# Loading q, k and v by whole batches instead of half batches in a fused sliding-window attention and soft-MoE kernel

## The chip, the cores and the metric

One core of a Trainium2 chip runs the whole kernel. The metric is the device time of one execution in microseconds (us); lower is better. Verdicts are ratios: the mean time of one kernel's fast runs divided by the mean time of the other's fast runs of the same rounds, with a 95% interval. They are therefore not quite the ratio of the medians that are quoted beside them. A profile is one execution; single executions of the same kernel differ, mostly by up to about 0.5%.

## The reference

Eight batches of eight heads, 576 tokens, head size 64. Each token attends to itself and the 63 tokens before it. The result, as 4608 rows of 512, goes through a soft mixture of eight experts with four slots each.

```python
def reference(q, k, v, phi, w1, w2):                  # cut and joined
    scores = scale * q @ k.T                          # per batch and head
    scores = where((rel >= 0) & (rel < 64), scores, -1e9)
    attn = softmax(scores) @ v                        # (8, 8, 576, 64)
    x = attn.transpose(0, 2, 1, 3).reshape(4608, 512)
    logits = x @ phi                                  # (4608, 32)
    slot_in = softmax(logits, axis=0).T @ x           # 32 slots
    for e in range(8):                                # 4 slots each
        slot_out[e] = relu(slot_in[e] @ w1[e]) @ w2[e]
    return softmax(logits, axis=1) @ slot_out
```

The inputs are float32 in HBM: 28.3 MB of q, k and v and 33.6 MB of weights. The output is 9.4 MB.

## The kernel before

The kernel works in 16 units of half a batch (four heads). All q, k, v and weight loads but the first three are DMAs issued by GpSimd, which cast float32 to float16 on the way (the software queue, q0). A partition of SBUF takes nine consecutive tokens of one head:

```python
    T = 9
    pld = ctx.enter_context(tc.tile_pool(name="pld", bufs=3))
    ...
    def src_of(u, i):
        b, half = units[u]
        return (q, k, v)[i][b, 4 * half:4 * half + 4].rearrange(
            "(x h) (g t) d -> (h g) x (t d)", x=2, h=2, t=T)

    def load_part(u, i):
        ...
        t = pld.tile([128, 2, S], FP16, name=nm, tag=nm)
        if u:                                            # unit 0 comes by the SP queue
            nc.gpsimd.dma_start(out=t, in_=src_of(u, i))  # 128 x 2 runs of 9*64 values
```

Each run of 9 x 64 values is one DMA packet of 1152 bytes (counted where it is written, in float16). The TensorEngine then transposes the tokens (stage `t1`), computes scores, and so on. The expert weights follow in the same queue; those of the last two experts' w2 come by column halves, so that the first half of the output columns can be combined and stored while the second half is still loading:

```python
            for _ in range(2 if u % 4 == 3 else 1):      # weights between the units
                load_w(*w_order.pop(0))
    ...
            if e > E - NLAST:
                stir(8)                                  # warming matmuls while PE waits
            expert_o(e, 0)
```

The softmax here doesn't subtract the row's maximum and nothing guards it: scores larger than these inputs give would overflow.

## Time and profile before

| | before |
|---|---|
| time, median | 181.57 us in the first 4 runs, 181.61 us in 16 runs with the later ones |
| span of the profiled run | 179.5 us |
| software queue | 22496 packets, 30.09 MB, 6.0 to 154.9 us |
| q, k, v packets of 1152 bytes | 11520 |
| attention done, experts begin | 133 us |
| last weight lands | 155.2 us |
| last store packet ends | 178.2 us |

The page of the kernel before, from the views of forty equal slices (busy share in tenths; GB/s is what all DMA engines moved) and of DMA queues (packets, MB, summed time of the packet records as a share of 16 engines' span):

```profile
...
PE   2559879968998797999978999887879947698200
...
DMA  5999999999999999999999999999999999999994
GB/s 199 287 209 202 206 210 212 208 205 213 209 213 202 209 213 208 209 207 210 211 205 213 207 213 206 213 213 218 205 217 214 204 196 179 332 376 408 429 422 183
...
q0 software_dynamic: 22496, 30.09, 94.8%
q1 hardware_dynamic: 6000, 11.21, 16.5%
q8 instruction: 23, 0.38, 0.8%
...
```

The DMA row is full in all but the edge slices; PE is nearly full too up to slice 30, but it ends attention in time and then waits. Loads run at some 209 GB/s, stores (slices 37 to 39) at 408 to 429.

The windows view of the same run, three stretches in which q, k, v and weights stream in:

```profile
...
core 0: us, PE busy (x) PEld busy (x) DVE busy (x) ACT busy (x) POOL busy (x), PEclk, DMA share, GB/s
20.00:60.00 40.00, 35.48 (x887) 27.43 (x885) 30.95 (x72) 32.48 (x53) 16.40 (x24) 1.00 1.17 209
60.00:100.00 40.00, 34.87 (x839) 26.66 (x838) 30.37 (x68) 31.52 (x55) 15.56 (x23) 1.00 1.16 209
100.00:130.00 30.00, 26.71 (x606) 20.08 (x607) 23.67 (x55) 21.78 (x38) 8.83 (x14) 1.00 1.13 211
...
```

The DMA share is above 1: the records of neighbouring packets on one engine overlap, so a record's length is not what a packet costs. That is the point on which the prediction turns.

The chain of work that ended last, in order of time (start us, length us, what):

```profile
...
98.47 13.99 DMA kn<-in_k_dram
112.75 19.50 DMA w2s<-in_moe_w_dram
132.53 0.88 POOL w2s L89
...
135.03 20.18 DMA w2l<-in_moe_w_dram
155.25 0.42 PE sop L522 x8
...
```

From 98 us the chain is DMA alone. Every load waits for 13 to 20 us behind about eight others in the queue; the last one lands at 155.2, and the matmul that waited for it runs at 155.25. Before 98 us the chain runs mostly through compute on PE, ACT and DVE, but the DMA row is full there too: with some eight loads in the queue, a load that is issued a little later doesn't leave the DMA engines idle.

### The profile page before, as it was taken

What the parts mean: (1) busy time and instruction counts of PE and PEld (TensorE: products, weight loads), DVE (VectorE), ACT (ScalarE), POOL (GpSimd) and SP (SyncE); (2) the same over time, 40 slices, a digit from 0 to 9 for tenths busy, and PEclk for the clock granted to TensorE, in tenths of its full rate; (3) what the DMA queues carried; (4) which work ended last, traced back from release to release, by engine and by line L of the source; (5) the groups of instructions that cost most, each with busy time, mean ns of one, the idle gap of its engine ahead of it and who ended that gap; (6) DMA issues with size and microseconds to landing.
All of it is one profiled execution on the core that took longest, in us unless ns stands there. A gap on an engine that the chain in (4) does not pass through costs nothing.

```text
span 179.5 us, 6676 instructions
## 1 busy us (share of the span) xinstructions
PE 139.8 (78%) x2929; PEld 102.1 (57%) x2929; DVE 114.1 (64%) x274; ACT 116.4 (65%) x203; POOL 55.2 (31%) x86
## 2 busy tenths in 40 slices
PE   2559879968998797999978999887879947698200
PEld 0448658647765676766757767675657724343000
DVE  5634969858949668886777886887842212589400
ACT  3556779787696777968769779694642313689400
POOL 8644534434343442524344333322131000000000
PEclk9999999999999999999999999999999997969955
DMA  5999999999999999999999999999999999999994
GB/s 199 287 209 202 206 210 212 208 205 213 209 213 202 209 213 208 209 207 210 211 205 213 207 213 206 213 213 218 205 217 214 204 196 179 332 376 408 429 422 183
DMA packets 28524, 41.71 MB, mean 232 GB/s; under 512 B 2128, under 2 KB 21584, under 8 KB 28496
## 3 DMA queue, kind: packets, MB, share of 16 engines
q0 software_dynamic: 22496, 30.09, 94.8%
q1 hardware_dynamic: 6000, 11.21, 16.5%
q8 instruction: 23, 0.38, 0.8%
q14 instruction: 5, 0.04, 0.1%
HBM read 61.93 MB, written 9.44 MB: 398 GB/s over the span
## 4 chain that ended last, share of the span: by engine, by line
DMA 34%; PE 34%; ACT 15%; issue 6%; DVE 3%; SPq 0%; POOL 0%; ACTq 0%; POOLq 0%
DMA w2l<-in_moe_w_dram 11%; DMA w2s<-in_moe_w_dram 11%; PE tr L164 10%; DMA kn<-in_k_dram 8%; ACT pm L227 5%; DMA first<-in_v_dram 4%; PE sc L215 4%; PE tr L193 4%; PE sc L222 4%; ACT ob L553 4%; PE tr L290 3%; PE av L253 3%; PE cp L549 3%; ACT kT L171 2%; PE lt L383 2%
## 5 line engine op out<-in xcount | busy, mean ns | idle before, releaser
L227 ACT ACTIVATE pm<-sc 128x1024 f16<-128x1024 f32 (+1 forms) x48 | 40.1, 835 | 18.6 <-PE sc L222 18.5
L215 PE MATMUL sc<-rep,hide 64*128 64x512 f16 (+1 forms) x96 | 18.1, 340 | 6.3 <-ACT pm L227 3.8
L261 DVE TENSOR_TENSOR x_bp<-av,rc 128x512 f16<-128x512 f32 x32 | 22.1, 690 | 1.0
L253 PE MATMUL av<-vw,pm 128*64 128x65 f16 x576 | 19.5, 197 | 3.7 <-issue 3.5
L171 ACT COPY qT<-tr 128x640 f16<-128x640 f16 (+1 forms) x31 | 21.2, 745 | 1.3 <-PE tr L164 1.3
L171 ACT COPY kT<-tr 128x640 f16<-128x640 f16 (+1 forms) x31 | 21.8, 785 | 0.2 <-PE tr L164 0.2
L222 PE MATMUL sc<-qT,kT 64*128 64x64 f16 x576 | 19.0, 193 | 0.6 <-issue 0.5
L555 DVE TENSOR_SCALAR ob<-cp,crcp 128x256 f32<-128x256 f32 (+1 forms) x25 | 13.9, 588 | 8.0 <-PE cp L549 7.9
L253 PEld LDWEIGHTS <-pm 128*64 128x64 f16 x576 | 16.0, 112 | 4.6 <-issue 3.9
L222 PEld LDWEIGHTS <-kT 64*128 64x128 f16 x576 | 15.4, 96 | 5.2 <-issue 1.4
L259 DVE RECIPROCAL rc<-av 128x8 f32<-128x8 f32 x32 | 6.4, 201 | 15.7 <-PE av L253 15.7
L66 POOL DMA_DIRECT2D vn<-in_v_dram x15 | 10.8, 720 | 15.3 <-PE sc L222 3.4
L553 ACT ACTIVATE ob<-cp,crcp 128x256 f32<-128x256 f32 (+1 forms) x26 | 13.7, 563 | 2.6 <-PE cp L549 1.7
L66 POOL DMA_DIRECT2D qn<-in_q_dram x15 | 10.8, 719 | 14.9 <-PE tr L204 4.0
L86 POOL DMA_DIRECT2D w1s<-in_moe_w_dram x16 | 8.8, 552 | 20.3 <-DMA w2s<-in_moe_w_dram 12.7
L549 PE MATMUL cp<-slot_oa,ET 128*128 128x256 f16 (+1 forms) x51 | 12.7, 348 | 2.8 <-ACT ob L553 1.1
L169 DVE COPY vT<-tr 128x512 f16<-128x512 f16 x16 | 11.6, 722 | 5.2 <-PE tr L164 5.2
L164 PE MATMUL tr<-ident,kn 128*64 128x128 f16 x288 | 13.7, 234 | 1.3 <-issue 1.2
L164 PE MATMUL tr<-ident,vn 128*64 128x128 f16 x288 | 12.6, 228 | 2.5 <-ACT vn L432 2.5
L66 POOL DMA_DIRECT2D kn<-in_k_dram x15 | 10.8, 718 | 11.1 <-PE tr L164 4.4
L171 ACT COPY vT<-tr 128x640 f16<-128x640 f16 x16 | 12.9, 809 | 1.5 <-PE tr L164 1.5
L164 PE MATMUL tr<-ident,qn 128*64 128x128 f16 x288 | 12.1, 233 | 1.7 <-ACT qn L432 1.7
(109 smaller groups left out, 241.5 us busy)
## 6 DMA issues: line engine op xcount, KB each, us to landing
w1s<-in_moe_w_dram POOLq DMA_DIRECT2D x16, 512.0 KB, 14.8
w2s<-in_moe_w_dram POOLq DMA_DIRECT2D x14, 512.0 KB, 14.8
out_dram<-ob SPq DMA_DIRECT2D x6, 768.0 KB, 7.5
qn<-in_q_dram POOLq DMA_DIRECT2D x15, 288.0 KB, 13.0
kn<-in_k_dram POOLq DMA_DIRECT2D x15, 288.0 KB, 13.0
vn<-in_v_dram POOLq DMA_DIRECT2D x15, 288.0 KB, 13.0
out_dram<-ob SPq DMA_DIRECT2D x8, 384.0 KB, 4.8
w2l<-in_moe_w_dram POOLq DMA_DIRECT2D x2, 512.0 KB, 19.9
```

Of the source, the lines that this page charges most:

```text
L66: nc.gpsimd.dma_start(out=t, in_=src_of(u, i))
L164: nc.tensor.transpose(tr[64 * x:64 * x + 64, j, :], src[:, x, 64 * (t0 + j):64 * (t0 + j) + 64], ident[:, :])
L169: nc.vector.tensor_copy(out=o, in_=i)
L171: nc.scalar.copy(out=o, in_=i)
L215: nc.tensor.matmul(sc[:, x, 0:128 * n], hide[64 * x:64 * x + 64, :], rep[64 * x:64 * x + 64, 0:2 * n, :], start=True, stop=False, skip_gro ...
L222: nc.tensor.matmul(sc[:, x, o:o + 64], st["kT"][64 * x:64 * x + 64, h, 64 * i:64 * i + 128], st["qT"][64 * x:64 * x + 64, h, 64 * i:64 * i ...
L227: nc.scalar.activation(pm[:, :, 0:2 * n, :], sc[:, :, 0:128 * n].rearrange("p x (w q) -> p x w q", q=64), AF.Exp, scale=scale)
L253: nc.tensor.matmul(av[r0:r0 + 64, kk, 65 * (w // 2):65 * (w // 2) + 65], pm[:, x, h * n + w, :], st["vw"][:, i, 2 * h + x, 0:65], start=Tr ...
L261: nc.vector.tensor_tensor(out=xb[:, c0:c0 + 2, 256 * half:256 * half + 256].rearrange("p c (k d) -> p k c d", d=64), in0=avv[:, :, :, 0:64 ...
L549: nc.tensor.matmul(cp[:, :], ET[:, bp, j::T], slot_oa[:, cols], start=True, stop=True)
L553: nc.scalar.activation(ob[:, g, :], cp[:, :], AF.Copy, scale=cr)
L555: nc.vector.tensor_scalar(out=ob[:, g, :], in0=cp[:, :], scalar1=cr, scalar2=None, op0=ALU.mult)
```

## The change

The change loads a whole batch at a time: 18 tokens of one head per partition, so a packet is 2304 bytes and there are half as many. Half as many DMAs are issued as well. The rest of the diff follows from that: two batches of buffers instead of three units, transposes by batch, a permuted order of the heads in x (undone in phi and in one final add), half-size w2 tiles that take over the freed buffers, and more warming matmuls near the end. The core of the diff, cut:

```diff
     T = 9            # still used for the first batch and the output
+    T2 = 18
-    pld = ctx.enter_context(tc.tile_pool(name="pld", bufs=3))
+    pld = ctx.enter_context(tc.tile_pool(name="pld", bufs=2))
...
-    def load_part(u, i):
-        t = pld.tile([128, 2, S], FP16, name=nm, tag=nm)
-            nc.gpsimd.dma_start(out=t, in_=src_of(u, i))
+    def load_batch(b):
+        for i in range(3):
+            t = pld.tile([128, 2, T2 * 64], FP16, name=names[i], tag=names[i])
+            nc.gpsimd.dma_start(out=t, in_=(q, k, v)[i][b].rearrange(
+                "(x h) (g t) d -> (h g) x (t d)", x=2, t=T2))
...
+        elif n >= 2 and (e, n - 2) not in w2_t:
+            tag = names[(2 * (e - E + 4) + n - 2) % 3]      # late w2 halves reuse q, k, v buffers
+            w2_t[e, n - 2] = pld.tile(...)
...
-            if u + 1 < nu:
-                stage_t1(u + 1, j)
+            if u == 0:
+                stage_t1_unit(1, j)                         # second half of batch 0
+            elif u == 1:
+                stage_t1(1, 2 * j)                          # all of batch 1 in one unit
+                stage_t1(1, 2 * j + 1)
+            elif b < B:
+                stage_t1(b, 3 * (u % 2) + j)
...
-            if e > E - NLAST:
-                stir(8)
+            if e >= E - NLAST:
+                stir(16 if e == E - 1 else 8)
```

(The comments are added here.)

More of the change, by code (lines that the diff above doesn't have):

```diff
@@ L34 @@
     T = 9
-    G = S // T
+    T2 = 18
     NW = S // 64
@@ L38 @@
     NFC = F // 128
+    PERM = (0, 2, 1, 3)
     scale = 1.0 / float(Dh) ** 0.5
@@ L42 @@
     gap.tile([128, 64], FP16, name="gap")
-    pld = ctx.enter_context(tc.tile_pool(name="pld", bufs=3))
+    pld = ctx.enter_context(tc.tile_pool(name="pld", bufs=2))
     pxb = ctx.enter_context(tc.tile_pool(name="pxb", bufs=2))
     pw1 = ctx.enter_context(tc.tile_pool(name="pw1", bufs=8))
-    pw2 = ctx.enter_context(tc.tile_pool(name="pw2", bufs=7))
+    pw2 = ctx.enter_context(tc.tile_pool(name="pw2", bufs=E - 4))
     const = ctx.enter_context(tc.tile_pool(name="const", bufs=1))
@@ L54, with src0, w2_of @@
     units = [(b, half) for b in range(B) for half in range(2)]
+    nu = len(units)
     loaded = {}
-    def src_of(u, i):
-        b, half = units[u]
-        return (q, k, v)[i][b, 4 * half:4 * half + 4].rearrange(
-            "(x h) (g t) d -> (h g) x (t d)", x=2, h=2, t=T)
-    def load_part(u, i):
-        nm = ("qn", "kn", "vn")[i]
-        t = pld.tile([128, 2, S], FP16, name=nm, tag=nm)
-        if u:
-            nc.gpsimd.dma_start(out=t, in_=src_of(u, i))
-        loaded[u, i] = t
-    def load_unit(u):
+    names = ("qn", "kn", "vn")
+    def src0(half, i):
+        return (q, k, v)[i][0].rearrange("(x r h) (g t) d -> r (h g) x (t d)", x=2, r=2, t=T)[half]
+    def load_batch(b):
         for i in range(3):
-            load_part(u, i)
+            t = pld.tile([128, 2, T2 * 64], FP16, name=names[i], tag=names[i])
+            nc.gpsimd.dma_start(out=t, in_=(q, k, v)[i][b].rearrange(
+                "(x h) (g t) d -> (h g) x (t d)", x=2, t=T2))
+            loaded[b, i] = t
     w1_t, w2_t = {}, {}
     NLAST = 2
+    def w2_of(e, f, cols):
+        if e >= E - NLAST:
+            return w2_t[e, cols.start // (D // 2)][:, f, :]
+        return w2_t[e, f // 4][:, f % 4, cols]
     def load_w(e, n):
@@ L78, in load_w @@
             w1_t[e] = pw1.tile([128, NHD, F], FP16, name="w1s", tag="w1s")
-        if n == 2:
-            if e < E - 1:
-                w2_t[e] = pw2.tile([128, NFC, D], FP16, name="w2s", tag="w2s")
-            else:
-                w2_t[e] = pxb.tile([128, NFC, D], FP16, name="w2l", tag="x_bp")
+        cols = e >= E - NLAST
+        if n == 2 and (e < E - 4 or e == E - 1):
+            if e < E - 4:
+                t = pw2.tile([128, NFC, D], FP16, name="w2s", tag="w2s")
+            else:
+                t = pxb.tile([128, NFC, D], FP16, name="w2l", tag="x_bp")
+            for m in range(2):
+                w2_t[e, m] = t[:, :, D // 2 * m:D // 2 * m + D // 2] if cols else t[:, 4 * m:4 * m + 4, :]
+        elif n >= 2 and (e, n - 2) not in w2_t:
+            tag = names[(2 * (e - E + 4) + n - 2) % 3]
+            w2_t[e, n - 2] = pld.tile([128, NFC, D // 2] if cols else [128, NFC // 2, D], FP16,
+                                      name="w2h", tag=tag)
         if n < 2:
@@ L86, in load_w @@
             nc.gpsimd.dma_start(out=w1_t[e][:, c], in_=moe_w1[e].rearrange("(p c) f -> p c f", p=128)[:, c])
-        elif e >= E - NLAST:
+        elif cols:
             c = slice(D // 2 * (n - 2), D // 2 * (n - 1))
-            nc.gpsimd.dma_start(out=w2_t[e][:, :, c], in_=moe_w2[e].rearrange("(c p) d -> p c d", p=128)[:, :, c])
+            nc.gpsimd.dma_start(out=w2_t[e, n - 2], in_=moe_w2[e].rearrange("(c p) d -> p c d", p=128)[:, :, c])
         else:
             g = slice(2 * n - 4, 2 * n - 2)
-            nc.gpsimd.dma_start(out=w2_t[e].rearrange("p (g c) d -> p g (c d)", c=2)[:, g],
+            nc.gpsimd.dma_start(out=w2_t[e, n - 2].rearrange("p (g c) d -> p g (c d)", c=2),
                                 in_=moe_w2[e].rearrange("(g p c) d -> p g (c d)", p=128, c=2)[:, g])
@@ L104 @@
         first.append(pw1.tile([128, 2, S], FP32, name="first", tag="w1s"))
-        nc.sync.dma_start(out=first[i], in_=src_of(0, i))
+        nc.sync.dma_start(out=first[i], in_=src0(0, i))
     ident = const.tile([128, 128], FP16, name="ident")
@@ L116 @@
     nc.vector.tensor_copy(out=hide[64:128, :], in_=m)
-    load_unit(0)
-    load_unit(1)
+    for i in range(3):
+        loaded[0, i] = pld.tile([128, 2, 2, T * 64], FP16, name=names[i], tag=names[i])
+        nc.gpsimd.dma_start(out=loaded[0, i][:, 1], in_=src0(1, i))
     rep = const.tile([128, 8, 64], FP16, name="rep")
@@ L128 @@
     for n in range(2):
-        kt = const.tile([128, 2, 64 + S], FP16, name=f"kT{n}")
-        vt = const.tile([128, 2, 64 + S], FP16, name="vT") if n == 0 else vTs[0]
+        kt = const.tile([128, 4, 64 + S], FP16, name=f"kT{n}")
+        vt = const.tile([128, 4, 64 + S], FP16, name="vT") if n == 0 else vTs[0]
         vw = const.tile([128, NW, 4, 66], FP16, name=f"vw{n}")
-        for h in range(2):
+        for h in range(4):
             nc.vector.memset(kt[:, h, 0:64], 0.0)
@@ L157, with t1 @@
     ps = psum1.enter_context(tc.tile_pool(name="ps", bufs=2, space=bass.MemoryType.PSUM))
-    def t1(src, dst, engines):
-        for (t0, n), eng in zip(((0, 5), (5, 4)), engines):
+    def t1(src, dst, pieces, engines):
+        nh = dst.shape[1]
+        nt = src.shape[2] // 64
+        for (t0, n), eng in zip(pieces, engines):
             tr = ps.tile([128, 8, 128], FP16, name="tr", tag="tr", bufs=4)
@@ L165, in t1 @@
                                         src[:, x, 64 * (t0 + j):64 * (t0 + j) + 64], ident[:, :])
-            o = dst.rearrange("p h (g t) -> p h g t", t=T)[:, :, :, t0:t0 + n]
-            i = tr[:, 0:n, :].rearrange("p t (h g) -> p h g t", h=2)
+            o = dst.rearrange("p h (g t) -> p h g t", t=nt)[:, :, :, t0:t0 + n]
+            i = tr[:, 0:n, :].rearrange("p t (h g) -> p h g t", h=nh)
             if eng is nc.vector:
@@ L173, with t1_dst, stage_t1_unit, stage_t1 @@
     state = {}
-    def stage_t1(u, which):
-        if which == 0:
-            qT = pqt.tile([128, 2, S], FP16, name="qT", tag="qT")
-            state[u] = dict(qT=qT, kT=kTs[u % 2], vT=vTs[u % 2], vw=vws[u % 2])
-            t1(loaded[u, 0], qT, (nc.scalar, nc.scalar if u else nc.vector))
-        elif which == 1:
-            t1(loaded[u, 1], state[u]["kT"][:, :, 64:64 + S], (nc.scalar, nc.scalar if u else nc.vector))
-        else:
-            t1(loaded[u, 2], state[u]["vT"][:, :, 64:64 + S], (nc.scalar, nc.vector))
+    byb = {}
+    def t1_dst(b, which):
+        if b not in byb:
+            byb[b] = (pqt.tile([128, 4, S], FP16, name="qT", tag="qT"), kTs[b % 2], vTs[b % 2])
+        return byb[b][which][:, :, 64:64 + S] if which else byb[b][which]
+    def stage_t1_unit(u, which):
+        engines = (nc.scalar, nc.vector) if u == 0 or which == 2 else (nc.scalar, nc.scalar)
+        t1(loaded[0, which][:, u], t1_dst(0, which)[:, 2 * u:2 * u + 2], ((0, 5), (5, 4)), engines)
+    def stage_t1(b, n):
+        which, part = divmod(n, 2)
+        engines = (nc.scalar, nc.vector) if which == 2 or b == 1 and part == 1 else (nc.scalar, nc.scalar)
+        if b == 1 and n == 4:
+            engines = (nc.vector, nc.vector)
+        t1(loaded[b, which], t1_dst(b, which), ((9 * part, 5), (9 * part + 5, 4)), engines)
+    def open_unit(u):
+        b, half = units[u]
+        qT, kT, vT = byb[b]
+        r = slice(2 * half, 2 * half + 2)
+        state[u] = dict(qT=qT[:, r], kT=kT[:, r], vT=vT[:, r], vw=vws[u % 2])
     def steps(j):
@@ L212, in stage_s @@
         n = len(wins)
-        sc = ps.tile([128, 2, 512], FP32, name="sc", tag="sc", bufs=1)
+        apart = False
+        if apart:
+            sc = [ps.tile([128, 512], FP32, name=f"sc{x}", tag="tr", bufs=4) for x in range(2)]
+        else:
+            sct = ps.tile([128, 2, 512], FP32, name="sc", tag="sc", bufs=1)
+            sc = [sct[:, x] for x in range(2)]
         for x in range(2):
-            nc.tensor.matmul(sc[:, x, 0:128 * n], hide[64 * x:64 * x + 64, :],
+            nc.tensor.matmul(sc[x][:, 0:128 * n], hide[64 * x:64 * x + 64, :],
                              rep[64 * x:64 * x + 64, 0:2 * n, :], start=True, stop=False,
@@ L221, in stage_s @@
                     o = 64 * (h * n + w)
-                    nc.tensor.matmul(sc[:, x, o:o + 64],
+                    nc.tensor.matmul(sc[x][:, o:o + 64],
                                      st["kT"][64 * x:64 * x + 64, h, 64 * i:64 * i + 128],
@@ L226, in stage_s @@
         pm = ppm.tile([128, 2, 8, 64], FP16, name="pm", tag="pm")
-        nc.scalar.activation(pm[:, :, 0:2 * n, :],
-                             sc[:, :, 0:128 * n].rearrange("p x (w q) -> p x w q", q=64),
-                             AF.Exp, scale=scale)
+        if apart:
+            for x in range(2):
+                nc.scalar.activation(pm[:, x], sc[x][:, :].rearrange("p (w q) -> p w q", q=64),
+                                     AF.Exp, scale=scale)
+        else:
+            nc.scalar.activation(pm[:, :, 0:2 * n, :],
+                                 sct[:, :, 0:128 * n].rearrange("p x (w q) -> p x w q", q=64),
+                                 AF.Exp, scale=scale)
         st["pm", j] = pm
@@ L332, in fin_ex @@
             for kk in range(NHD):
-                nc.tensor.matmul(fin["sums"][:, 1, NSLOT * c:NSLOT * c + NSLOT], fin_x(b, kk, c), phi_sb[:, kk, :],
+                nc.tensor.matmul(fin["sums"][:, 1, NSLOT * c:NSLOT * c + NSLOT], fin_x(b, kk, c), phi_sb[:, PERM[kk], :],
                                  start=(kk == 0), stop=(kk == NHD - 1))
@@ L354, in fin_lt @@
             x = moe[b][:, kk, 2 * part:2 * part + 2] if part < 2 else moe[b, 8][:, kk]
-            nc.tensor.matmul(fin["lt", part], phi4[:, kk].rearrange("p r s -> p (r s)"), x,
+            nc.tensor.matmul(fin["lt", part], phi4[:, PERM[kk]].rearrange("p r s -> p (r s)"), x,
                              start=(kk == 0), stop=(kk == NHD - 1))
@@ L382, in stage_logit @@
         for kk in range(NHD):
-            nc.tensor.matmul(lt[:, :], phi4[:, kk].rearrange("p r s -> p (r s)"), moe[b][:, kk],
+            nc.tensor.matmul(lt[:, :], phi4[:, PERM[kk]].rearrange("p r s -> p (r s)"), moe[b][:, kk],
                              start=(kk == 0), stop=(kk == NHD - 1))
@@ L388, in stage_logit @@
             for kk in range(NHD):
-                nc.tensor.matmul(l8[:, :], phi4[:, kk].rearrange("p r s -> p (r s)"), moe[b, 8][:, kk],
+                nc.tensor.matmul(l8[:, :], phi4[:, PERM[kk]].rearrange("p r s -> p (r s)"), moe[b, 8][:, kk],
                                  start=(kk == 0), stop=(kk == NHD - 1))
@@ L414, in stage_slot @@
             nc.vector.tensor_tensor(out=acc[:, :], in0=pa[:, :], in1=acc[:, :], op=ALU.add)
-    nu = len(units)
     w_order = [(e, n) for e in range(E - NLAST) for n in range(4)]
@@ L421, in issue_loads @@
     def issue_loads(u):
-        if u + 3 < nu:
-            load_unit(u + 3)
-            for _ in range(2 if u % 4 == 3 else 1):
-                load_w(*w_order.pop(0))
+        if u == 1 or u > 1 and u % 2 == 0:
+            b = u // 2 + 2
+            if b < B:
+                load_batch(b)
+                for _ in range(2 + b % 2):
+                    load_w(*w_order.pop(0))
+            else:
+                for _ in range(len(w_order) if u > nu - 4 else 8):
+                    load_w(*w_order.pop(0))
+    load_batch(1)
     load_w(*w_order.pop(0))
-    load_unit(2)
     todo = []
@@ L431 @@
         if which < 3:
-            nc.scalar.copy(out=loaded[0, which][:, 0], in_=first[which][:, 0])
-            nc.vector.tensor_copy(out=loaded[0, which][:, 1], in_=first[which][:, 1])
+            nc.scalar.copy(out=loaded[0, which][:, 0, 0], in_=first[which][:, 0])
+            nc.vector.tensor_copy(out=loaded[0, which][:, 0, 1], in_=first[which][:, 1])
         else:
-            stage_t1(0, which - 3)
+            stage_t1_unit(0, which - 3)
     nc.vector.tensor_copy(out=phi4, in_=phi_sb.unsqueeze(2).broadcast_to([128, NHD, 4, NSLOT]))
     first_part.close()
+    MAN = 4
     pend = None
@@ L440 @@
         issue_loads(u)
-        if u == nu - 3:
-            while w_order:
-                load_w(*w_order.pop(0))
+        open_unit(u)
         for j in range(3):
@@ L451 @@
             stage_s(u, j)
-            if u + 1 < nu:
-                stage_t1(u + 1, j)
+            b = u // 2 + 1
+            if u == 0:
[5 more added lines that the diff above has]
+                stage_t1(b, 3 * (u % 2) + j)
             if pend is not None:
@@ L469 @@
     b = B - 1
-    with tc.manual_schedule(engines={mybir.EngineType.PE, mybir.EngineType.Activation, mybir.EngineType.DVE}):
-        stage_s(nu - 1, 2)
-        fin_xt(b, 0)
-        stage_av(nu - 1, 1)
-        fin_ex(b, (0, 1))
-        stage_av(nu - 1, 2, own=True)
-        fin_xt(b, 1)
-        fin_slot(b, (0, 1))
-        fin_xt(b, 2)
-        fin_lt(b, 0)
-        fin_ex(b, (2, 3, 4))
-        fin_lt(b, 1)
-        fin_slot(b, (2, 3, 4))
-        nc.vector.tensor_tensor(out=pa_sb[:, :], in0=fin["sums"][:, 0, :], in1=acc[:, :], op=ALU.add)
-        fin_lt(b, 2)
-        for part in range(3):
-            fin_et(b, part)
+    last_part = ExitStack()
+    last_part.enter_context(tc.manual_schedule(
+        engines={mybir.EngineType.PE, mybir.EngineType.Activation, mybir.EngineType.DVE}))
+    stage_s(nu - 1, 2)
+    fin_xt(b, 0)
+    stage_av(nu - 1, 1)
+    fin_ex(b, (0, 1))
+    stage_av(nu - 1, 2, own=True)
+    fin_xt(b, 1)
+    fin_slot(b, (0, 1))
+    fin_xt(b, 2)
+    fin_lt(b, 0)
+    fin_ex(b, (2, 3, 4))
+    fin_lt(b, 1)
+    fin_slot(b, (2, 3, 4))
+    nc.vector.tensor_tensor(out=pa_sb[:, :].rearrange("p (x r c) -> p r x c", x=2, r=2),
+                            in0=fin["sums"][:, 0, :].rearrange("p (r x c) -> p r x c", x=2, r=2),
+                            in1=acc[:, :].rearrange("p (r x c) -> p r x c", x=2, r=2), op=ALU.add)
+    fin_lt(b, 2)
+    for part in range(3):
+        fin_et(b, part)
+    last_part.close()
     psum1.close()
@@ L522, in expert_o @@
                 nc.tensor.matmul(sop[half][32 * g:32 * g + 32, :], hT[:, 4 * i + g, :],
-                                 w2_t[e][:, 4 * i + g, halves[half]],
+                                 w2_of(e, 4 * i + g, halves[half]),
                                  start=(e == 0 and i == 0), stop=(e == E - 1 and i == NFC // 4 - 1))
@@ L580 @@
                 expert_t(e + 1)
-            if e > E - NLAST:
-                stir(8)
+            if e >= E - NLAST:
+                stir(16 if e == E - 1 else 8)
             expert_o(e, 0)
```

## The prediction

> **What bounds the kernel now.** The 16 DMA engines. In the page's forty slices the DMA row is 9 in all but the first and the last; the software queue (loads that cast f32 to f16, issued by GpSimd) moves 30.09 MB from 6.0 to 154.9 us. The issues take 13 to 15 us to landing although a q, k or v transfer alone needs about 1.4 us, so some eight are always in flight: the queue never runs dry. PE is busy about 90% of 40 to 120 us (the windows view: 36.0 of 40 us), a close second, but attention ends near 132 us, and from 144 us PE waits for the last weights (the chain of waits: w2s, then w2l, landing at 155.2). Then come 24 us of output stores, at 389 GB/s between 156 and 178 us, also DMA.
>
> **What the change does.** Attention is loaded a whole batch at a time: 18 tokens per partition instead of 9, so 1152-byte packets become 2304 bytes, and 45 DMAs become 24. The bytes are the same. Transposes, copies, matmuls and exponentials keep number and shapes; they only move (two units' loads are transposed in unit 1, none in unit 14). The permuted head order costs nothing. Two batches of buffers take the place of three units; the last w2 halves reuse them. Eight, then sixteen warming matmuls precede the last experts, where PE waits for DMA anyway.
>
> **Cost.** In the packet records a 1152-byte packet takes 107 ns, 2048 bytes 173, 4096 bytes 324: 22 ns plus 0.0737 ns a byte. It would be tempting to save 22 ns on each of 5376 merged pairs: 7.4 us. But records of neighbouring packets overlap (the DMA share in these stretches is 1.2, not 1.0). A fit of packet counts to elapsed time from 13 to 152 us gives 88.6 ns for 1152 bytes, 41.3 for 512, 154.8 for 2048, 305.6 for 4096: 3.7 ns a packet plus 0.0737 ns a byte, and about 16 ns for the closing packet of a DMA on each engine. The Trainium skill ("DMA: Bandwidth & Descriptors", Why small descriptors are slow) tells of some 3 cycles per packet inside the engine; the fitted 3.7 ns is that small. My estimate is then 173.5 ns for 2304 bytes against 177.2 for two of 1152: 5376 x 3.7 ns / 16 = 1.2 us, plus 21 DMAs x 16 ns = 0.3 us: 1.5 us, all on the critical path, as the DMA stream is continuous.
>
> **Where it could be given back.** Batch b+2 can load once the transposes of batch b have freed its buffers. By my count of the stream the data land 2 to 5 us before they are needed and each buffer is free 10 us or more before its transfer's turn, so the stream should stay full. The tail doesn't change: its packets are the stores'.
>
> **Predicted time:** 180.0 us, 8 in 10 between 178.4 and 181.4. Faster by over 2%: 0.10; within 2%: 0.86; slower: 0.04.
>
> **What would show the steps right.** The last q, k, v packet lands near 103 us instead of 114.5 (weights go behind it); software queue packets drop by 5376 plus 336 closing ones; its summed packet time falls by over 7 us (its share of 16 engines to about 91%) while elapsed time falls by only some 1.5 us; the rate in q, k, v stretches rises from 203 to about 210 GB/s; the last w2l lands near 153.7; the tail stays at 24 us.
>
> **What would make it wrong.** Gaps in the DMA row where GpSimd waits for a buffer; 2304-byte packets off the line through the other sizes; sixteen warming matmuls that hold back the first stores; PE, 90% busy, falling behind in unit 1 with the doubled transposes.

## The result, and the profile after

The changed kernel took 180.44 us (median of 11 runs, 179.64 to 180.67) against 181.61 us (16 runs). The ratio is 0.9923, interval 0.9908 to 0.9938: a small, certain gain, which is 1.4 us of 181.61 (0.0077 x 181.61). A second set of runs gave 0.9918.

The same two views of the page, after:

```profile
...
PE   0669879997889998879999898987879987888200
...
DMA  5999999999999999999999999999999999999994
GB/s 176 311 206 212 213 212 214 211 211 211 217 212 209 212 212 213 212 212 213 213 212 211 214 212 212 214 211 213 213 214 215 200 197 162 346 362 416 421 421 170
...
q0 software_dynamic: 16784, 30.08, 90.8%
q1 hardware_dynamic: 6000, 11.21, 16.5%
q8 instruction: 23, 0.38, 0.8%
...
```

5712 packets are gone from q0 (22496 - 16784: 5376 merged data packets and 336 closing packets), the bytes are the same, and the DMA row is as full as before: no gap has opened. The summed time of q0's records fell from 94.8% of 179.5 to 90.8% of 178.7 us, which is 7.9 us. The kernel gained only 1.4.

The same windows, after:

```profile
...
core 0: us, PE busy (x) PEld busy (x) DVE busy (x) ACT busy (x) POOL busy (x), PEclk, DMA share, GB/s
20.00:60.00 40.00, 35.56 (x865) 27.75 (x861) 31.70 (x71) 35.00 (x52) 10.56 (x17) 1.00 1.10 212
60.00:100.00 40.00, 36.03 (x875) 27.97 (x873) 31.06 (x69) 35.54 (x58) 9.60 (x15) 1.00 1.10 212
100.00:130.00 30.00, 26.02 (x578) 19.33 (x575) 24.66 (x57) 20.55 (x34) 7.59 (x12) 1.00 1.10 213
...
```

The DMA share fell from 1.17 to 1.10: the records overlap less. The rate, which is what counts, rose from 209 to 212 GB/s, 1.4%. Two more lines of the windows moved: ACT is busier (32.5 to 35.0 of 40 us) and GpSimd much less so (16.4 to 10.6), as it issues fewer DMAs. The DMA row stays full beside both.

The chain that ended last, after:

```profile
...
89.92 20.75 DMA w2s<-in_moe_w_dram
...
111.22 20.30 DMA w2h<-in_moe_w_dram
...
131.80 0.87 POOL w2h L98
...
135.54 18.91 DMA w2l<-in_moe_w_dram
154.49 0.64 PE sop L572 x7
...
```

It is the same chain of loads, and it ends 0.8 us sooner: the matmul that waited for the last weight runs at 154.49 instead of 155.25. From there the kernel needs 24.2 us to the end of its span, as before (178.7 - 154.49 against 179.5 - 155.25).

A group of PSUM copies on ACT and two kinds of DMA issues (KB each, then the median us from issue to landing), before and then after:

```profile
...
L171 ACT COPY kT<-tr 128x640 f16<-128x640 f16 (+1 forms) x31 | 21.8, 785 | 0.2 <-PE tr L164 0.2
...
w2s<-in_moe_w_dram POOLq DMA_DIRECT2D x14, 512.0 KB, 14.8
...
qn<-in_q_dram POOLq DMA_DIRECT2D x15, 288.0 KB, 13.0
...
```

```profile
...
L183 ACT COPY kT<-tr 128x640 f16<-128x640 f16 (+1 forms) x30 | 23.6, 877 | 0.2 <-PE tr L176 0.2
...
w2s<-in_moe_w_dram POOLq DMA_DIRECT2D x8, 512.0 KB, 20.8
qn<-in_q_dram POOLq DMA_DIRECT2D x7, 576.0 KB, 20.5
...
```

The copies of transposed k became slower (785 to 877 ns; 788 to 903 ns for the 128x640 shape alone). Their destination is now a 4 x 32 x 5 pattern instead of 2 x 64 x 5; that this is the cause was not tested. The prediction said that the copies keep their shapes; the counts agree, the pattern of the destination does not. ACT had room for it. The issues now land after about 20.5 us instead of 13 to 15: some eight loads are still in flight, and each is now larger. A longer wait in a queue that never runs dry costs nothing.

### The profile page after: what moved, and what is told of

It reads as the page before. It is cut to its first block, busy times and chain, and to the rows that moved or that the text cites. A ratio compares the mean times of both kernels' runs of the same rounds, so it can differ in the third digit from the quotient of the medians.

```text
span 178.7 us, 6673 instructions
## 1 busy us (share of the span) xinstructions
PE 140.6 (79%) x2945; PEld 103.7 (58%) x2945; DVE 117.2 (66%) x283; ACT 121.9 (68%) x200; POOL 40.3 (23%) x65
## 3 DMA queue, kind: packets, MB, share of 16 engines
q0 software_dynamic: 16784, 30.08, 90.8%
## 4 chain that ended last, share of the span: by engine, by line
DMA 50%; PE 21%; ACT 13%; issue 5%; DVE 4%; SPq 0%; POOL 0%; ACTq 0%; POOLq 0%
DMA kn<-in_k_dram 12%; DMA w2s<-in_moe_w_dram 12%; DMA w2h<-in_moe_w_dram 11%; DMA w2l<-in_moe_w_dram 11%; PE tr L176 6%; DMA first<-in_v_dram 4%; ACT ob L603 4%; ACT pm L262 4%; ACT qT L183 3%; PE tr L218 3%; DVE vT L181 3%; PE cp L599 3%; PE sc L245 2%; PE sc L252 2%; PE tr L325 2%
## 5 line engine op out<-in xcount | busy, mean ns | idle before, releaser
L183 ACT COPY qT<-tr 128x640 f16<-128x640 f16 (+1 forms) x30 | 23.4, 860 | 1.4 <-PE tr L176 1.3
L183 ACT COPY kT<-tr 128x640 f16<-128x640 f16 (+1 forms) x30 | 23.6, 877 | 0.2 <-PE tr L176 0.2
L176 PE MATMUL tr<-ident,qn 128*64 128x128 f16 x288 | 13.4, 234 | 7.6 <-ACT qn L472 5.2
L181 DVE COPY vT<-tr 128x512 f16<-128x512 f16 (+1 forms) x17 | 13.9, 834 | 7.8 <-PE tr L176 7.7
L176 PEld LDWEIGHTS <-qn 128*64 128x64 f16 x288 | 9.9, 116 | 9.7 <-ACT qn L472 5.2
L183 ACT COPY vT<-tr 128x640 f16<-128x640 f16 x15 | 14.0, 932 | 0.9 <-PE tr L176 0.9
L218 PE MATMUL tr<-ident,vT 128*128 128x128 f16 x128 | 10.5, 224 | 3.3 <-issue 2.0
L219 DVE COPY vw<-tr 128x1024 f16<-128x1024 f16 x16 | 11.0, 688 | 3.2 <-PE tr L218 3.1
L176 PE MATMUL tr<-ident,kn 128*64 128x128 f16 x288 | 12.1, 228 | 0.2
L599 PEld LDWEIGHTS <-ET 128*128 128x128 f16 x51 | 7.0, 142 | 8.7 <-issue 6.7
## 6 DMA issues: line engine op xcount, KB each, us to landing
w1s<-in_moe_w_dram POOLq DMA_DIRECT2D x16, 512.0 KB, 20.5
qn<-in_q_dram POOLq DMA_DIRECT2D x7, 576.0 KB, 20.5
```

The costliest lines, as they stand in the source:

```text
L176: nc.tensor.transpose(tr[64 * x:64 * x + 64, j, :], src[:, x, 64 * (t0 + j):64 * (t0 + j) + 64], ident[:, :])
L181: nc.vector.tensor_copy(out=o, in_=i)
L183: nc.scalar.copy(out=o, in_=i)
L218: nc.tensor.transpose(tr[:, 2 * w + h, :], vT[:, h, 64 + 128 * w:192 + 128 * w], ident[:, :])
L599: nc.tensor.matmul(cp[:, :], ET[:, bp, j::T], slot_oa[:, cols], start=True, stop=True)
```

## The experiments

Theory: the stream of loads bounds the kernel, and a packet costs a fixed 3.7 ns beside its bytes (0.0737 ns a byte), so that the 5376 packets saved are worth 1.2 us and the DMAs saved another 0.3 us. Rivals: (a) the number of DMAs, not of packets, is what counts; (b) reordered work, buffers or warming matmuls bring the gain; (c) a packet costs the 22 ns of its record, and the missing 6 us are lost somewhere else.

Beside the times there is a second, sharper measure, worked out from each trace. The 16 DMA engines do not finish together (see below). At a moment when all of them are still busy with the last weight packets of 4096 bytes, the packets still to come times 305.6 ns, divided by 16, give the time at which the average engine will be done with that part of the stream. I call it the average engine's end. Choosing that moment a few us earlier or later moves the result by less than 0.1 us.

| kernel | packet, DMAs of batches 1 to 7 | average engine's end, us | time, median us | ratio to before, 95% |
|---|---|---|---|---|
| before | 1152 | 142.55 | 181.61 | 1 |
| changed | 2304, 21 | 140.94 | 180.44 | 0.9923 [0.9908, 0.9938] |
| changed again | 2304, 21 | 141.00 | 180.53 | 0.9918 [0.9892, 0.9945] |
| xsplit | 2304, 42 | 141.38 | 180.67 | 0.9948 [0.9922, 0.9974] |
| pad1152 | 1152, 42 | 142.55 | 181.73 | 1.0015 [0.9985, 1.0046] |
| pad768 | 768, 42 | 143.77 | 183.49 | 1.0110 [1.0068, 1.0152] |
| pad384 | 384, 42 | 147.37 | 188.15 | 1.0357 [1.0339, 1.0375] |

### The changed kernel again

No edit.

> The changed kernel unaltered, as the base for the runs beside it. Every theory: ratio to the kernel before 0.992, some 1.4 us faster.

180.53 us, ratio 0.9918. As expected.

### xsplit: the packets of the change, twice the DMAs

```diff
-            nc.gpsimd.dma_start(out=t, in_=(q, k, v)[i][b].rearrange(
-                "(x h) (g t) d -> (h g) x (t d)", x=2, t=T2))
+            for x in range(2):
+                nc.gpsimd.dma_start(out=t[:, x], in_=(q, k, v)[i][b, 4 * x:4 * x + 4].rearrange(
+                    "h (g t) d -> (h g) (t d)", t=T2))
```

> Each q, k, v load of a batch is issued as two DMAs, one for each half of the free dimension: packets stay 2304 bytes, the DMAs of batches 1 to 7 go from 21 to 42. Packet theory (the gain is 3.7 ns for each packet saved): only the closing packets come back, 336 of 16 to 20 ns over 16 engines, 0.3 to 0.4 us more than the changed kernel, ratio to before 0.994. Rival (the gain comes from the halved number of DMAs and their issue): nearly all of the 1.4 us comes back, ratio 0.999 or more.

Ratio 0.9948. The average engine ended 0.4 us later than with the change whole (141.38 against 140.94 and 141.00). The halved number of DMAs is therefore the smaller part of the gain, about a quarter by this measure (0.0030 x 181.6 = 0.5 us in the timed rounds, with intervals that overlap), and rival (a), which expected 0.999 or more, falls. The Trainium skill ("DMA: Bandwidth & Descriptors", Anatomy of one DMA) gives a fixed cost of some 2 us for one such DMA; 21 more of them cost 0.4 us in all here, 20 ns each: with about eight in flight and the DMA row full, that latency does not add up.

### pad1152: the packets of before in the changed kernel

```diff
-            t = pld.tile([128, 2, T2 * 64], FP16, ...)
+            t = pld.tile([128, 2, 2, T2 // 2 * 64 + 32], FP16, ...)   # a gap splits each run in two
+            for x in range(2):
+                nc.gpsimd.dma_start(out=t[:, x, :, 0:T2 // 2 * 64], in_=(q, k, v)[i][b, 4 * x:4 * x + 4].rearrange(
+                    "h (g s t) d -> (h g) s (t d)", s=2, t=T2 // 2))
```

The transposes read the same tokens at their new places. (One DMA with this gap for both x does not build: its pattern has more than three dimensions. Hence the comparison with xsplit.)

> As xsplit, and the destination has a gap of 64 bytes between the two runs of nine tokens, so every packet is 1152 bytes again; batches, order, buffers, warming matmuls as in the changed kernel. Packet theory: 5376 packets more x 3.7 ns / 16 = 1.2 us more than xsplit, ratio to before 1.000 to 1.002. Rival (reordered work, buffers or warming matmuls bring the gain): same as xsplit, ratio 0.994 or less. Rival (a packet costs the 22 ns of its record): 7.4 us more than xsplit, ratio 1.035.

Ratio 1.0015: the whole gain is gone, with the changed kernel's batches, order, buffers and warming matmuls all in place. The average engine ended 1.17 us later than in xsplit, and the timed rounds differ by as much (0.0067 x 181.6 = 1.2 us). Rivals (b) and (c) fall. The gap in the destination doesn't seem to be the cause: the kernel before has packets of this length without a gap, and its average engine ends at the same 142.55 us.

### pad768 and pad384: still shorter packets

The same edit with three runs of six tokens and with six runs of three.

> As pad1152 with three runs of six tokens: packets of 768 bytes. Packet theory: another 5376 packets, another 1.2 us, ratio to before 1.007 to 1.009. Rival 22 ns: ratio 1.075. Rival (order, buffers): 0.994.

> As pad768 with six runs of three tokens: packets of 384 bytes. Packet theory with 3.7 ns a packet: 3 x 5376 packets more than pad768, 3.7 us more, ratio about 1.03; with the step that pad1152 and pad768 showed in the timed runs (1.8 us) up to 1.04. Rival: the straight line ends at short packets, and the ratio is well above 1.04.

The average engine's end moved by another 1.22 us for the next 5376 packets, and by 3.60 us for 16128 more, 1.20 us for each 5376. Times 16 engines and divided by 5376, that is 3.5, 3.6 and 3.6 ns a packet: one constant from 2304 bytes down to 384. A fit of packet counts to elapsed time in pad384 gives 31.9 ns for a 384-byte packet (30.8 to 31.4 when it is repeated with slices of 1 to 4 us), where the line of the prediction gives 3.7 + 0.0737 x 384 = 32.0.

The timed steps were somewhat larger than the stream's (pad768 over pad1152: 0.0095 x 181.6 = 1.7 us, with a wide interval; pad384 over pad768: 0.0247 x 181.6 = 4.5 us against 3.6 expected from the stream). pad768 lies above the 1.007 to 1.009 that was expected, though its interval reaches down to it. In pad384's trace the rest is visible behind the stream: 24.4 us pass from its last load packet to its last store packet, 23.4 in pad768. Why is left open.

The windows view of xsplit, pad1152 and pad768 (the columns as in the windows above; the last two are DMA share and GB/s), and the line of q0 of each:

```profile
...
20.00:60.00 40.00, 35.89 (x879) 28.19 (x874) 32.33 (x71) 35.49 (x53) 13.79 (x24) 1.00 1.10 211
60.00:100.00 40.00, 35.93 (x864) 27.80 (x864) 31.16 (x69) 35.38 (x57) 12.60 (x22) 1.00 1.10 212
...
```

```profile
...
q0 software_dynamic: 17120, 30.09, 91.2%
...
```

```profile
...
20.00:60.00 40.00, 36.08 (x893) 28.59 (x887) 32.57 (x72) 35.48 (x53) 16.09 (x24) 1.00 1.16 209
60.00:100.00 40.00, 36.10 (x860) 27.85 (x859) 30.81 (x69) 35.51 (x57) 15.16 (x23) 1.00 1.16 209
...
```

```profile
...
q0 software_dynamic: 22496, 30.09, 94.7%
...
```

```profile
...
20.00:60.00 40.00, 36.15 (x897) 28.52 (x891) 32.82 (x72) 35.44 (x53) 16.92 (x24) 1.00 1.23 207
60.00:100.00 40.00, 35.93 (x859) 27.70 (x859) 31.21 (x69) 35.33 (x57) 15.95 (x23) 1.00 1.22 207
...
```

```profile
...
q0 software_dynamic: 27872, 30.09, 98.2%
...
```

pad1152 shows the kernel before's 22496 packets, share 1.16 and 209 GB/s. PE and ACT do in it what they do in xsplit, so the rate of the stream moves with the packets alone. And q0's summed records, 91.2, 94.7 and 98.2%, times the spans of 178.4, 179.6 and 181.2 us, rise by 7.4 and 7.9 us, where the average engine's end moves by 1.2 us each time.

### oldstir: the warming matmuls of before

```diff
-            if e >= E - NLAST:
-                stir(16 if e == E - 1 else 8)
+            if e > E - NLAST:
+                stir(8)
```

> The changed kernel with the warming matmuls of the kernel before (eight ahead of the last expert, none ahead of the last but one). Packet theory: no effect on the end of the loads, ratio to before 0.992 as with the change whole. Rival (the added warming matmuls keep the TensorE clock up and give a part of the gain): 0.995 or more; rival (they hold back the first stores): 0.990 or less.

Ratio 0.9935 [0.9913, 0.9957], median 180.40 against 180.53 for the changed kernel. It was run at another time. The better comparison lies in the same call: spnops, which turned out to be the changed kernel unaltered (see below), took 180.03 us, 0.9915 [0.9899, 0.9931]. The intervals overlap, so the added warming matmuls are worth nothing that these runs can show, though a loss of 0.2% without them is not excluded. They do what they are meant to do: the windows view shows a granted clock of 0.77 from 144 to 150 us before, 0.69 in oldstir and 1.00 in the changed kernel. But PE waits for loads there, and the average engine ends at 140.9 us in oldstir as with the change whole.

### w2row and w2row_phihw: an attempt at a better version

If packets cost 3.7 ns, the 4096 packets of 512 bytes for the last two w2 are the next thing to merge. w2row loads only the last expert's w2 by column halves:

```diff
-        cols = e >= E - NLAST
+        cols = e >= E - 1
...
-    ... [(e, n) for n in range(2, 4) for e in last]
+    ... [(e, n) for e in last for n in range(2, 4)]
...
-            if e < E - NLAST:
+            if e < E - 1:
                 expert_o(e, 1)
```

> Towards a better version: only the last expert's w2 is loaded by column halves (512-byte packets), that of the last but one by row pairs (2048 bytes): 2048 packets of 41.2 ns become 512 of 154. Packet theory: 0.34 us less in the stream, 0.2 to 0.4 us less in all, ratio 0.990, unless the first stores, which can start 2.6 us later, leave the DMA engines idle; then 0.992 to 0.996.

> As w2row, and phi (512 packets of 64 bytes, 27 ns each in the software queue, 0.86 us over 16 engines) is loaded as float32 through the SP queue behind the first loads and cast by DVE. Packet theory: another 0.3 to 0.6 us less, ratio 0.987.

Both were slower than the kernel before: 183.26 us, 1.0074, and 183.54 us, 1.0073. My expectation was wrong on both. The windows around the end of the loads, of the changed kernel and then of w2row:

```profile
...
150.00:154.00 4.00, 3.53 (x23) 1.93 (x22) 2.67 (x6) 2.75 (x8) 0.00 (x0) 0.76 0.99 221
154.00:158.00 4.00, 3.23 (x20) 1.87 (x19) 2.27 (x5) 2.71 (x7) 0.00 (x0) 0.50 1.02 355
...
```

```profile
...
150.00:154.00 4.00, 3.33 (x23) 1.95 (x22) 0.40 (x1) 0.92 (x3) 0.00 (x0) 0.58 0.50 68
154.00:158.00 4.00, 3.13 (x23) 2.01 (x23) 3.12 (x8) 3.53 (x9) 0.00 (x0) 1.00 0.81 282
...
```

From 150 to 154 us the DMA share in w2row is 0.50, at 68 GB/s, against 0.99 and 221. The first store packet came at 154.8 us instead of 151.8, after the last load packet (153.7), so the engines had nothing to do. The last store ended 26.6 us after the last load, where the changed kernel needs 23.2. I had named this danger but put it at a loss of up to 0.4% against the changed kernel; it cost about 1.5%. The split by column halves buys overlap, and the 512-byte packets are its price. Moving phi to the other queue gained nothing on top: its 512 packets, then of 128 bytes, have records of 26 ns there, against 27 ns in q0.

### nlast3: the opposite

```diff
-    NLAST = 2
+    NLAST = 3
```

(and the warming matmuls kept before the last two experts only)

> The opposite of w2row: the last three experts' w2 come by column halves (512-byte packets), so the first stores can start some 2.6 us earlier, while the load stream grows by 0.34 us. Theory (the slowest DMA engine ends its loads, then needs 23.2 us for its share of the stores, and the first stores of the changed kernel already come early enough): no gain, 0.2 to 0.4 us more than the changed kernel, ratio 0.993 to 0.995, and the stores end 23.2 us after the last load. Rival (the time runs from the first store, as in w2row): 2 us less than the changed kernel, ratio 0.981.

```profile
...
150.00:154.00 4.00, 2.35 (x25) 1.27 (x25) 2.25 (x6) 2.52 (x6) 0.00 (x0) 1.00 1.20 283
154.00:158.00 4.00, 1.04 (x11) 0.61 (x11) 0.01 (x1) 0.37 (x1) 0.00 (x0) 0.77 0.79 269
...
```

181.11 us, 0.9958 [0.9939, 0.9976]: some 0.35% or 0.6 us slower than the changed kernel, although the first store packet came at 150.4 us, 1.3 us earlier. The direction is the theory's; the size is above its 0.2 to 0.4 us, with an interval that reaches into its range. The rival, that the time runs from the first store, falls. My number for the tail was off: the last load ended at 156.1 us because early stores shared the engines with it, and the stores ended 22.0 us later, not 23.2. From 154 to 158 us the DMA share is 0.79: the stores of the first column half had run out before the second half could be computed. Two experts by column halves is the best of the three settings tried.

### spnops: more instruction fetches, which were not there

This was meant to test how instruction fetches delay single DMA engines (next section): 2048 empty instructions on the idle SP engine.

```diff
+    for _ in range(2048):
+        nc.sync.nop(nofuse=True)
```

> The changed kernel with 2048 empty instructions on the idle SP engine after the first loads, about eight more 16 KB instruction fetches. Lag theory (each such fetch holds one of the 16 DMA engines for some 1.05 us and that engine never catches up, so the slowest engine sets the landing of every load): about eight more fetch packets in the trace; the mean engine ends its loads 0.5 us later, the slowest up to 1 us later; ratio to before 0.995 to 0.999. Rival (a fetch only takes its share of a common pool, or delays nobody): 0.992 to 0.995, and the spread of the landings over the 16 engines no wider than 3.6 to 4.6 us.

The trace has 23 fetch packets and 6673 instructions, just as without the edit: the empty instructions are not in the program that ran. The run says nothing about added fetches; it is one more repeat of the changed kernel (180.03 us, 0.9915), and as such it will be of use in the next section. I found no other edit that adds fetches without also loading an engine that matters, so that question stays untested.

## Why the prediction was right

- **Bound.** The DMA row stays full, and the same chain of loads ends the kernel's first 154 us. Shown by the profile after, and by the pad runs, in which only packet length moves the time.
- **Cost of a packet.** The prediction took 3.7 ns from a fit of counts to elapsed time and set aside the 22 ns that the records suggest. Measured by the three steps of the ladder: 3.5, 3.6 and 3.6 ns. The fit of the changed kernel's own trace gives 173.3 ns for 2304 bytes, where the prediction said 173.5; but repeated with slices of 1 to 4 us it gives 168 to 173, with an uncertainty of 2 to 3 ns, too coarse to check a constant of 3.7 ns. The ladder is the check. The tempting calculation, 7.4 us, is just what the summed records show (7.9 us less), and it is not time.
- **Cost of a DMA.** 0.3 us predicted for 21 DMAs; the average engine shows 0.4 in xsplit.
- **Sum.** 1.5 us predicted in all. The average engine's end moved by 1.6 us (142.55 to 140.94 and 141.00), the timed rounds by 1.4 us. The predicted time was 180.0, the measured median 180.44, within the range; the ratio 180.0 / 181.57 = 0.991 lies within the measured interval.
- **Nothing given back.** No slice of the DMA row opened, so two batches of buffers were enough.
- **Signs that were off.** The last q, k, v packet ended at 105.4 us, not near 103. The rate rose from 209 to 212 GB/s over long stretches, which hold weights too; where over 97% of the bytes are q, k and v it rose from 205.5 to 209.3 GB/s (20 to 104 us, in slices of 1 us), against the 203 to 210 expected. The last weight packet ended at 154.17 us, 0.7 us earlier, where I had expected 1.5. This last one deserves a reason.

**Where the profiled run hid half of the gain.** A load's semaphore rises by 16 as it lands, once for each engine, as the Trainium skill says ("DMA: Bandwidth & Descriptors", Why a DMA increments its semaphore by 16 and not by 1); the trace has 16 such events for each of these loads. Sorted, they tell how far each engine lags behind the first. Four loads of the changed kernel (time of the first engine's landing, then the lag of all 16, us):

```
 11.61  0.0  0.04 0.06 0.11 0.12 0.16 0.21 0.23 0.24 0.29 0.30 0.32 0.33 0.37 0.61 1.23
 64.83  0.0  0.05 0.20 0.32 0.34 0.35 0.62 0.67 1.12 1.30 1.34 1.38 1.40 1.42 1.74 3.47
109.69  0.0  0.26 0.32 0.33 0.40 0.41 0.65 1.21 2.20 2.38 2.42 2.45 2.47 2.48 2.80 5.01
149.91  0.0  0.26 0.32 0.33 0.40 0.40 0.95 1.21 2.21 2.37 3.54 3.56 3.58 3.59 3.92 4.54
```

The engines start nearly together and drift apart, mostly by steps of about 1.1 us, and the steps keep pace with the packets of q8, the instruction queue: 23 packets of 16 KB, one about every 6 us, each with a record of 0.88 to 0.98 us. Between the first and the last of these four loads the 16 lags grow by 26.6 us in sum, and 22 such packets start: 1.2 us for each. I read this so: an engine that carries one is late from then on. The table shows no engine that catches up to the first while the loads run. A load lands when its slowest engine is done. In the kernel before, the slowest engine was 3.6 us behind the first at 141 us; in the changed kernel 4.5 us at 139 us (4.6 in the repeat). So the average engine gained 1.6 us in the profiled pair, and the slowest only 0.7. In xsplit the lag is 3.7 us, and its last load ended at 153.80 us, before the changed kernel's 154.17, although its stream is longer. And in spnops, which is the changed kernel once more, the lag is 3.6 us and the last weight packet ends at 153.38 us: 1.5 us earlier than in the kernel before, just the step that the prediction gave. The mean lag is 1.7 to 1.9 us in all of these traces at that time; what differs is how far the slowest engine is from it. That the fetches cause the steps is read from their timing and size in the traces; no experiment removed or added one, and the traces don't name the engine of a packet.

The end of the kernel follows the slowest engine: in eight traces (before, the changed kernel, its repeat, xsplit, pad1152, pad768, oldstir, spnops) the last store packet ends 23.2 to 23.4 us after the last load packet.

What stays open: the 17 runs of the changed kernel fall into two groups, 179.64 to 179.97 us (6 runs) and 180.21 to 180.71 us (11 runs). A different luck of the lags would give such a step. Only profiled executions show lags, and there are three of this program: 180.47 and 180.67 us with lags of 4.5 and 4.6 us, and 179.78 us (spnops) with 3.6. They fit, but three are few, and what decides the lag of the slowest engine is not known, so this is not shown.

No version beat the changed kernel.

## What to carry to other kernels

Don't take the length of a DMA record for the cost of a packet: where the DMA share of 16 engines is above 1, fit packet counts to elapsed time instead, and the fixed cost that longer packets can save may be a sixth of what the records suggest. Merging packets pays in a stream that is already full, but only by that small constant times their number; merging those that serve an overlap, such as column halves that let stores begin early, can lose more than it saves. A load lands with its slowest engine, so a change of 1 us should be judged from many timed runs or from the average engine, not from the last landing in one profile.

## What the Trainium skill lacked or had wrong

- "DMA: Bandwidth & Descriptors", Why small descriptors are slow: it tells of about 3 cycles per packet, but names no clock for them and says nothing of casting loads. Taken as cycles of the 850 MHz that the same page gives for the fabric (Where 436 GB/s comes from), they would be 3.5 ns, an estimate; the runs show 3.5 to 3.6 ns a packet from 2304 down to 384 bytes, and 0.0737 ns per byte written. The page doesn't say that the records are some 18 ns longer than that.
- "DMA: Bandwidth & Descriptors", Specifications: the bandwidth of an engine, about 27 GiB/s (29 GB/s), isn't tied to a side of a casting load. Here 0.0737 ns per float16 byte is 13.6 GB/s written and 27.1 GB/s read, so the figure fits only the float32 side, and better as 27 GB/s than as 27 GiB/s. No run loaded a full stream without a cast to confirm it.
- "DMA: Bandwidth & Descriptors", Anatomy of one DMA (2 us fixed) and the rule of at least 1 MiB a transfer (under Bandwidth): neither gives a figure for a queue with several loads in flight. With about eight, 21 more DMAs cost 0.4 us in all, 20 ns each.
- "Runtime: NRT & Kernel Launch", Instruction fetch mechanics: it calls the cost of crossing a 16 KiB block mostly hidden. The traces show packets of that size with records of about 1 us on the 16 DMA engines; by their timing they add up, in a full stream, to a lag of 3.6 to 4.6 us for the slowest engine, which sets when loads land. No experiment changed their number.
- "DMA: Bandwidth & Descriptors" says that engines 7 and 15 are usually slower than the others in traces, and of another case that a bulk load runs at the pace of its slowest engine. No page that I found says that the engines of a full stream drift apart step by step, nor that the last landing then differs from the average engine by over 2 us (here the slowest engine is 4.5 us behind the first, the mean 1.9).
